# An expert's last short block computed beside a pair of its blocks, in one group of 320 columns

## The chip, the cores and the metric

The kernel runs on one core of a Trainium2 chip. The metric is the device time of one execution in microseconds (us), the median of several runs. A profile of one execution is shown beside it, with the work of the five engines: TensorE (PE, with its weight loads as PEld), VectorE (DVE), ScalarE (ACT), GpSimd (POOL) and SyncE (SP, which issues most of the DMA transfers).

## The reference

A linear attention gives 4608 tokens of 512 numbers, and a mixture of eight experts works on them. Each token goes to one expert only. The change touches the expert part alone.

```
# attention: phi(x) = [exp(p), exp(-p)], p = x @ w_phi - max|x @ w_phi|;  x: [4608, 512]
logits = x @ w_gate                      # [4608, 8]
expert_idx = argmax(logits, axis=1)
gate_w = softmax(logits)[expert_idx]
for e in range(8):
    xe = x[expert_idx == e]
    h = maximum(xe @ w1[e], 0)           # w1[e]: [512, 1024]
    out[expert_idx == e] = gate_w * (h @ w2[e])   # w2[e]: [1024, 512]
```

With the reference's inputs the eight experts get 759, 439, 659, 402, 373, 412, 536 and 1028 tokens. In blocks of 128 that is 6, 4, 6, 4, 3, 4, 5 and 9 blocks, 41 in all. The last blocks hold 119, 55, 19, 18, 117, 28, 24 and 4 tokens.

## The kernel before

The first 400 us compute the attention and write its rows to `x_dram`, with the routing of the first 27 of 36 token tiles done on the way. The expert that has most tokens by then is the "lead" expert: its weights are loaded first and its first three blocks are gathered early. Then the last nine tiles are routed (`route` with `final`). `place` works out on VectorE where each expert's blocks stand, `block_of` turns that into a block number per token, `tokens_of` finds the token of each place by 72 small matmuls into `pp`, and `experts_of` finds the expert of each block (`eidx`). `gather` fetches a block's token rows from `x_dram` by an indirect DMA, issued on GpSimd.

Every fp32 product is made of three matmuls of rounded parts: high by high, low by high and high by low. `weights(u, k)` splits one of eight weight pieces of unit `u` (k 0 to 3 of `w1`, 4 to 7 of `w2`): ScalarE casts `raw` to `wh`, then VectorE (or GpSimd for k = 3 and 7) subtracts and writes `wl`. `load_weights` loads the raw piece by SyncE, and skips the transfer if the next unit has the same expert. `x_parts` transposes a gathered block on TensorE into `px` and splits it into `xh` and `xl`.

Blocks are computed in units. A **pair** is two blocks of one expert, 256 tokens. Its first product (`pair_first`, four steps j) has the weights as the stationary operand and 256 token columns moving, 96 matmuls in all into `pm`. ScalarE then writes `hh` (ReLU, rounded) and VectorE `hl`. Its second product (`pair_second`) has 128 tokens stationary and 512 output columns moving, 48 matmuls into two banks `po`. A **single** is one block: 24 matmuls with 512 moving columns (`first_product`), eight transposes of the hidden values (`h_parts`, into `pht`), and 24 matmuls with 512 columns (`second_product`). `write` scales `po` by the token's gate value on ScalarE and scatters the rows by an indirect DMA.

There are 17 pairs and then 7 singles in a row, 41 blocks; two more singles run only if the count of blocks asks for them. The singles are software-pipelined by `step`. In the attention the order of each engine is written out by hand. In the expert part it is not: a scheduler places the instructions of each engine, starting from the order of the code, and each engine then works through its own list in order.

Of the kernel before, what the change touches and what calls it, by code (L numbers as in the profile page):

```python
# [19 lines left out]
P = 128  # L20
# [13 lines left out]
NPAIR = 17  # L34
NU = NB - NPAIR
NU_ALWAYS = NU - 2

NSLOT = 7
# [46 lines left out]
def tile_linear_attention_moe(  # L85
# [20 lines left out]
    gidx = keep.tile([P, NB], I32, name="gidx")  # L106
    sidx = keep.tile([P, NB], I32, name="sidx")
# [514 lines left out]
    spot = sg.tile([P, E], F32, name="spot")  # L622

    def place(pc):
# [4 lines left out]
        V.tensor_scalar(cni, cni, 6, 2, op0=ALU.arith_shift_right, op1=ALU.bitwise_and)  # L629
# [3 lines left out]
        even, odd2 = pe[:, 0], pe[:, 1]  # L633
        V.tensor_copy(odd2, cni)
        V.scalar_tensor_tensor(even, odd2, -0.5, nb, op0=ALU.mult, op1=ALU.add)
        spare = sg.tile([P, 1], F32, name="spare")
        V.tensor_reduce(spare, even, axis=AX.X, op=ALU.add)
        V.tensor_scalar(spare, spare, -1.0, 2.0 * NPAIR, op0=ALU.mult, op1=ALU.add)
        st8 = sg.tile([P, 2, E, E], F32, name="st8")
# [10 lines left out]
        V.scalar_tensor_tensor(over, over, -0.5, nb, op0=ALU.mult, op1=ALU.add)  # L650
        V.tensor_scalar(spare, spare, 0.0, None, op0=ALU.max)
        V.scalar_tensor_tensor(first, pst[:, 1], spare, pst[:, 0], op0=ALU.min, op1=ALU.add)
        V.tensor_scalar(paired, first, -1.0, 2.0 * NPAIR, op0=ALU.mult, op1=ALU.add)
        V.scalar_tensor_tensor(paired, paired, 0.0, over, op0=ALU.max, op1=ALU.min)
        V.tensor_tensor(singles, nb, paired, op=ALU.subtract)
        V.tensor_tensor(st8[:, 0], before, singles.unsqueeze(1).to_broadcast([P, E, E]), op=ALU.mult)
        V.tensor_reduce(start, st8[:, 0], axis=AX.X, op=ALU.add)
        V.tensor_scalar_add(start, start, 2.0 * NPAIR)
        V.tensor_tensor(spot, start, paired, op=ALU.subtract)
        V.scalar_tensor_tensor(spot, spot, 64.0, paired, op0=ALU.mult, op1=ALU.add)  # L660
        V.scalar_tensor_tensor(spot, spot, 64.0, first, op0=ALU.mult, op1=ALU.add)
# [222 lines left out]
    def lead():  # L884
# [13 lines left out]
        def pick_lead():  # L898
# [8 lines left out]
            V.tensor_scalar(key, iota_em, ld, -2.0 * E, op0=ALU.is_equal, op1=ALU.mult)  # L907
            V.tensor_tensor(key, key, iota_e, op=ALU.add)
# [177 lines left out]
    def block_of():  # L1086
        si_t = spots.tile([P, NTILE, E], F32, name="si_t")
        at = spots.tile([P, NTILE], I32, name="at")
        V.tensor_tensor(si_t, onehot, spot.unsqueeze(1).to_broadcast([P, NTILE, E]), op=ALU.mult)
        with nc.allow_low_precision("places are integers"):  # L1090
            V.tensor_reduce(at, si_t, axis=AX.X, op=ALU.add)

        late_at = spots.tile([P, NTILE], I32, name="late_at")
        turn = spots.tile([P, NTILE], I32, name="turn")
        V.tensor_scalar(turn, at, 6, 63, op0=ALU.arith_shift_right, op1=ALU.bitwise_and)
        V.tensor_single_scalar(late_at, at, 12, op=ALU.arith_shift_right)
        V.tensor_single_scalar(at, at, 63, op=ALU.bitwise_and)
        bi = spots.tile([P, NTILE], F32, name="bi")
        V.tensor_tensor(bi, blk, turn, op=ALU.is_ge)
        V.tensor_tensor(late_at, late_at, at, op=ALU.subtract)  # L1100
        V.tensor_tensor(bi, bi, late_at, op=ALU.mult)
        V.tensor_tensor(blk, blk, at, op=ALU.add)
        V.tensor_tensor(bi, bi, blk, op=ALU.add)
        for j0 in range(0, NTILE, 12):
            V.tensor_tensor(
                bsel[:, j0 : j0 + 12, :],
                iota_p[:, 0:NB].unsqueeze(1).to_broadcast([P, 12, NB]),
                bi[:, j0 : j0 + 12].unsqueeze(2).to_broadcast([P, 12, NB]),
                op=ALU.is_equal,
            )  # L1110

    def tokens_of():

        pp = ps_kv.tile([P, NB], F32, name="pp", tag="pk")
# [4 lines left out]
        emp = spots.tile([P, NB], F32, name="emp")  # L1119
# [3 lines left out]
    def experts_of():  # L1123
        ends = spots.tile([1, 2, E], F32, name="ends")
        G.tensor_tensor(ends[:, 0], first[0:1], paired[0:1], op=ALU.add)
        G.tensor_tensor(ends[:, 1], start[0:1], singles[0:1], op=ALU.add)
        V.tensor_reduce(nblk, ends[:, 1], axis=AX.X, op=ALU.max)
        eg = spots.tile([1, 2, NB, E], F32, name="eg")
        places = ((first[0:1], ends[:, 0], 0, 2 * NPAIR), (start[0:1], ends[:, 1], 2 * NPAIR, NB))
        for low, high, n0, n1 in places:  # L1130
            for j, edge in enumerate((low, high)):
                m = V.tensor_tensor(
                    eg[:, j, n0:n1],
                    iota_p[0:1, n0:n1].unsqueeze(2).to_broadcast([1, n1 - n0, E]),
# [5 lines left out]
        G.tensor_tensor(eg[:, 0], eg[:, 0], iota_e[0:1].unsqueeze(1).to_broadcast([1, NB, E]), op=ALU.mult)  # L1140
        with nc.allow_low_precision("experts are integers"):
            V.tensor_reduce(eidx, eg[:, 0], axis=AX.X, op=ALU.add)
# [6 lines left out]

    def blocks(u):  # L1150
        return [2 * u, 2 * u + 1] if u < NPAIR else [u + NPAIR]
# [40 lines left out]
    def x_parts(u, i):  # L1192
        if u >= lim[0] or i >= len(blocks(u)) or ("x", u, i) in st:
            return
        if i == 0:
            st["x", u] = [mp.tile([P, KD, 2 * P], F32R, name=n) for n in ("xh", "xl")]
        st["x", u, i] = True
        xg = st["xg", blocks(u)[i]]
        px = ps_x.tile([P, KD, P], F32, name="px")
        for k in range(KD):  # L1200
            turn(px[:, k, :], xg[:, k * P : (k + 1) * P])
        xh, xl = (x[:, :, i * P : (i + 1) * P] for x in st["x", u])
        A.copy(xh, px)
        V.tensor_tensor(xl, px, xh, op=ALU.subtract)
# [6 lines left out]
    def pair_first(u, j, half=None):  # L1211

        xh, xl = st["x", u]
# [146 lines left out]
    for u in range(1, NPAIR):  # L1360
        for j in range(4):
            pair_first(u, j)
            if j > 1:
                x_parts(u + 1, j - 2)
# [113 lines left out]
```

## Time and profile before

| | us |
|---|---|
| median of 3 runs | 904.98 |
| the runs | 902.72 to 909.48 |
| the profiled execution | 898.09 |
| its span, first to last instruction | 896.4 |
| TensorE busy in that span | 865.8 (97%) |
| ScalarE, VectorE, GpSimd busy | 608.0, 580.1, 487.1 |

A busy time is the union of an engine's instructions, so TensorE at 97% says that it hardly ever had nothing to do. It does not say how long one matmul holds it: a matmul's own duration (0.28 us for 256 columns) overlaps with its neighbours'. What a matmul costs is the distance from its start to the next one's start.

### The profile page before, as it was taken

The numbers are of one execution on the slowest core, as the hardware profiler recorded it, in microseconds if no ns is written. First come the engines' busy times: TensorE is split into PE (matmuls) and PEld (weight loads), VectorE is DVE, ScalarE is ACT, GpSimd is POOL, SyncE is SP. The second block draws the span as 40 slices with busy tenths as digits, with TensorE's granted clock in tenths as the row PEclk, the third lists the DMA queues.
The fourth block names the chain that finished last, engine by engine and source line by source line (L and its number), as shares of the span: only waits on it lengthen the run. The fifth ranks groups of instructions, "written<-read, shape, count | busy, mean of one in ns | idle before, by whom it ended". The sixth has DMA issues, their size and how long they took to land. (4 is left out here: it accounts for less than half of the span.)

```text
span 896.4 us, 18565 instructions
## 1 busy us (share of the span) xinstructions
PE 865.8 (97%) x6639; PEld 806.9 (90%) x6639; DVE 580.1 (65%) x1073; ACT 608.0 (68%) x954; POOL 487.1 (54%) x332
## 2 busy tenths in 40 slices
PE   7989999999999999989999999999999999999994
PEld 6989999999999999988899999999999999987883
DVE  7878789777978778677945444444454445557950
ACT  6969788988898879564655555555555555568951
POOL 6877677876787768532533333333343433345631
PEclk7999999999999999999999999999999999999998
DMA  6556655565646545560251253422535634653100
GB/s 209 154 159 196 201 186 158 173 198 185 184 153 201 185 133 159 166 210 14 96 170 66 96 165 118 164 72 89 164 119 158 215 119 119 243 198 110 47 25 15
DMA packets 81262, 129.73 MB, mean 145 GB/s; under 512 B 13006, under 2 KB 32974, under 8 KB 81168
## 3 DMA queue, kind: packets, MB, share of 16 engines
q1 hardware_dynamic: 73776, 107.58, 38.2%
q0 software_dynamic: 6720, 20.80, 7.4%
q8 instruction: 53, 0.87, 0.4%
q14 instruction: 41, 0.34, 0.1%
q10 hardware_dynamic: 672, 0.15, 0.1%
HBM read 136.81 MB, written 20.26 MB: 175 GB/s over the span
## 5 line engine op out<-in xcount | busy, mean ns | idle before, releaser
L59 DVE TENSOR_TENSOR wl<-raw,wh 128x1024 fp32r<-128x1024 f32 x138 | 184.2, 1347 | 134.4 <-ACT wh L59 134.4
L59 ACT CAST wh<-raw 128x1024 fp32r<-128x1024 f32 x184 | 191.3, 1051 | 92.0 <-PE po L59 64.4
L59 POOL TENSOR_TENSOR wl<-raw,wh 128x1024 fp32r<-128x1024 f32 x46 | 112.5, 2450 | 176.3 <-ACT wh L59 163.4
L59 PE MATMUL pm<-xh,wh 128*128 128x256 f32 x544 | 154.3, 284 | 2.7 <-DVE hl L59 2.7
L59 PE MATMUL pn<-kf,qp 128*128 128x73 f32 x1024 | 156.6, 253 | 0.0
L59 PE MATMUL pm<-xl,wh 128*128 128x256 f32 x544 | 154.8, 285 | 1.4 <-DVE xl L59 1.4
L59 PE MATMUL pm<-xh,wl 128*128 128x256 f32 x544 | 154.4, 284 | 0.0
L59 PEld LDWEIGHTS pn<-kf,qp 128*128 128x128 f32 x1024 | 151.1, 190 | 0.1
L59 PE MATMUL po<-wh,hh 128*128 128x512 f32 x328 | 131.4, 401 | 0.9 <-ACT hh L59 0.9
L59 PE MATMUL po<-wh,hl 128*128 128x512 f32 x328 | 128.1, 390 | 0.6 <-DVE hl L59 0.6
L59 PE MATMUL po<-wl,hh 128*128 128x512 f32 x328 | 128.5, 392 | 0.0
L59 POOL TENSOR_TENSOR kl<-e,kh 128x1024 fp32r<-128x1024 f32 x47 | 112.8, 2407 | 24.6 <-ACT kh L59 23.6
L59 DVE TENSOR_REDUCE mx<-ps_proj 128x4 f32<-128x512 f32 (+1 forms) x160 | 99.6, 634 | 34.7 <-PE ps_proj L59 33.7
L59 POOL TENSOR_TENSOR xl<-xr,xh 128x512 fp32r<-128x512 f32 (+2 forms) x63 | 93.1, 1482 | 51.8 <-ACT xh L59 31.1
L59 PEld LDWEIGHTS pm<-xh,wh 128*128 128x128 f32 x544 | 104.7, 193 | 5.3 <-DVE hl L59 2.8
L59 PEld LDWEIGHTS pm<-xl,wh 128*128 128x128 f32 x544 | 104.8, 193 | 4.2 <-DVE xl L59 1.7
L59 PEld LDWEIGHTS pm<-xh,wl 128*128 128x128 f32 x544 | 104.8, 193 | 0.0
L59 DVE TENSOR_TENSOR t<-ps_proj,mx 128x512 f32<-128x512 f32 (+1 forms) x160 | 97.8, 630 | 2.0
L59 POOL DMA_INDIRECT out<-ob,sidx x41 | 43.5, 1061 | 91.0 <-ACT ob L59 80.1
L59 ACT ACTIVATE e<-t 128x512 f32<-128x512 f32 (+1 forms) x160 | 85.4, 592 | 8.1 <-DVE kl L59 3.4
L59 PE MATMUL ps_proj<-w_hi,xh 128*128 128x256 f32 x288 | 84.1, 294 | 6.3 <-DVE t L59 3.1
L59 DVE SCALAR_TENSOR_TENSOR hl<-pm,hh 128x512 fp32r<-128x512 f32 x68 | 46.7, 687 | 61.5 <-ACT hh L59 61.5
(206 smaller groups left out, 1989.3 us busy)
## 6 DMA issues: line engine op xcount, KB each, us to landing
raw<-w SPq DMA_DIRECT2D x184, 512.0 KB
tq<-t SPq DMA_DIRECT2D x64, 256.0 KB
vt<-vv SPq DMA_DIRECT2D x15, 640.0 KB
x_dram<-xrow SPq DMA_DIRECT2D x30, 256.0 KB
xr<-kT SPq DMA_DIRECT2D x15, 320.0 KB
xr<-qT SPq DMA_DIRECT2D x15, 320.0 KB
xr<-kT SPq DMA_DIRECT2D x17, 256.0 KB
xr<-qT SPq DMA_DIRECT2D x17, 256.0 KB
```

Of the source, the lines that this page charges most:

```text
L59: m = f(*a, **kw)
```

## The change

The units have three forms now: nine pairs (`p`), six **trios** (`t`) and five singles (`s`) that always run, in the order that `FORMS` gives; eight more singles run only if there are more than 35 blocks beside the short ones.

A trio is a pair of an expert's blocks and that expert's last block, if that holds at most 64 tokens. The first product moves 320 columns instead of 256, one bank `pm` per 128 hidden rows (`trio_first`). In the hidden tile `h2` the columns stand so that the 64 high values of the short block and its 64 low values are neighbours. In the second product (`trio_second`) those 128 columns are one stationary operand: one matmul with `th` and one with `tl` give, in the lower 64 rows of `po2`, the high part's result, and in the upper 64 rows the low part's. `write_half` adds the two halves: ScalarE copies the upper half of `po2` to SBUF, a DMA moves it to the lower partitions, VectorE adds, ScalarE scales, and the scatter writes 64 rows.

```
+FORMS = "pp" + "p" * (NPLAIN - 3) + "tp" + "ts" * NONE_ALWAYS + "s" * (NONE - NONE_ALWAYS)
-NSLOT = 7
+NSLOT = 6
...
+    def trio_first(u, j):
+        xh, xl = st["x", u]
+        n = 2 * P + HALF
+        for i in range(2):
+            f = 2 * (j % 2) + i
+            pm = ps_h.tile([P, n], F32, name="pm")
+            for k in range(KD):
+                th, tl = (w[:, f * P : (f + 1) * P] for w in first_weights(u, j // 2, k))
+                T.matmul(pm, th, xh[:, k, :], start=(k == 0), stop=False)
+                T.matmul(pm, th, xl[:, k, :], start=False, stop=False)
+                T.matmul(pm, tl, xh[:, k, :], start=False, stop=(k == KD - 1))
+            h2 = hidden("h2", 2 * n)
+            A.activation(h2[:, 0:n], pm, AF.Relu)
+            for o, t, m in ((n + HALF, 0, 2 * P), (n, 2 * P, HALF)):
+                V.scalar_tensor_tensor(
+                    h2[:, o : o + m], pm[:, t : t + m], 0.0, h2[:, t : t + m], op0=ALU.max, op1=ALU.subtract
+                )
+            st["h2", u, 2 * j + i] = h2
...
+            both = h2[:, 2 * P : 3 * P]
+            T.matmul(po2, both, th[:, c], start=first, stop=False)
+            T.matmul(po2, both, tl[:, c], start=False, stop=last)
...
+    def write_half(b, po):
+
+        lower, upper = slice(0, HALF), slice(HALF, P)
+        ob = op.tile([P, DM], F32, name="ob", bufs=4)
+        A.copy(ob[upper], po[upper])
+        nc.sync.dma_start(ob[lower], ob[upper])
+        V.tensor_tensor(ob[lower], po[lower], ob[lower], op=ALU.add)
+        A.activation(ob[lower], ob[lower], AF.Copy, scale=gates[lower, b : b + 1])
+        scatter(b, lower, ob)
...
+        else:
+            first_product(u, 0)
+            x_parts(u + 1, 0)
+            tail(u - 1, 0)
+            x_parts(u + 1, 1)
+            tail(u - 1, 1)
+            x_parts(u + 1, 2)
+            ahead_weights(u, 0)
+            first_product(u, 1)
+            ahead_weights(u, 1)
+            h_parts(u, 0)
+            ahead_weights(u, 2)
```

`place` gets more steps: it finds which experts have a short last block and at least two full blocks to stand beside (four more for the lead expert), takes the first six, and places pairs, trios and singles. Its result per expert is two packed words instead of one, so `block_of` multiplies, sums and unpacks twice. `gates` keeps the gate values of all blocks (one small copy per block on VectorE), the transposed blocks use two fixed banks (`px0`, and `px1`, which `po2` shares), and six slots instead of seven hold the split pieces of `w2`.

The order that the scheduler made moves at three places.

On VectorE, ahead of the 72 matmuls `pp`: before, one word is formed (`spot`), multiplied and summed (`si_t`, `at`) and unpacked, and then `bsel` is compared.

```order
L59 SCALAR_TENSOR_TENSOR spot<-spot,first 128x8
L59 TENSOR_TENSOR si_t<-onehot,spot 128x288
L59 TENSOR_REDUCE at<-si_t 128x36
L59 TENSOR_SCALAR turn<-at 128x36
L59 TENSOR_SCALAR late_at<-at 128x36
L59 TENSOR_TENSOR bi<-blk,turn 128x36
L59 TENSOR_SCALAR at<-at 128x36
L59 TENSOR_TENSOR late_at<-late_at,at 128x36
L59 TENSOR_TENSOR blk<-blk,at 128x36
L59 TENSOR_TENSOR bi<-bi,late_at 128x36
L59 TENSOR_TENSOR bi<-bi,blk 128x36
L59 TENSOR_TENSOR bsel<-iota_p,bi 128x516 x3
```

Of the change, the end of the same stretch (`b_...` are the fields of the second word):

```order
L65 TENSOR_TENSOR b_6484<-b_6484,first 128x8
L65 SCALAR_TENSOR_TENSOR spot<-b_6488,b_6485 128x8
L65 TENSOR_TENSOR blk<-blk,low 128x36
L65 TENSOR_REDUCE nblk<-ends 1x1
L65 SCALAR_TENSOR_TENSOR spot<-spot,b_6484 128x8
L65 TENSOR_TENSOR words<-onehot,spot 128x288
L65 TENSOR_REDUCE at<-words 128x36
L65 TENSOR_SCALAR move<-at 128x36 x3
L65 TENSOR_TENSOR past<-past,move 128x108
L65 TENSOR_REDUCE bi<-past 128x36
L65 TENSOR_TENSOR bi<-bi,blk 128x36
L65 TENSOR_TENSOR bsel<-iota_p,bi 128x588 x3
```

From the first step of `place` to the first `bsel`, without the splits of weights and values that stand between, VectorE's list holds 45 steps before and 79 now. On TensorE, 11 more matmuls `po` of the first unit stand ahead of `pp`, and 5 instead of 16 between `pp` and the transposes of the next gathered block.

On VectorE, in a single: before, the splits of the weights (`wl`), of the hidden values (`hl`) and of the next block (`xl`) alternate.

```order
L59 TENSOR_TENSOR wl<-raw_6286,wh 128x1024
L59 TENSOR_TENSOR hl<-pht,hh 128x512
L59 TENSOR_TENSOR wl<-raw_6288,wh 128x1024
L59 TENSOR_TENSOR hl<-pht,hh 128x512
L59 TENSOR_TENSOR xl<-px,xh 128x4x128
```

Of the change, a single that follows a trio (`po_9375` is the bank `po2` of that trio, `h_9704` a hidden tile `h2` of the next one):

```order
L65 TENSOR_TENSOR xl<-px,xh 128x4x64
L65 COPY gates<-xg 128x1
L65 TENSOR_TENSOR wl<-raw_6298,wh 128x1024
L65 TENSOR_TENSOR wl<-raw_6292,wh 128x1024
L65 TENSOR_TENSOR ob<-po_9375,ob 64x512
L65 TENSOR_TENSOR hl<-pht,hh 128x512
L65 SCALAR_TENSOR_TENSOR h_9704<-pm,h_9704 128x256
L65 SCALAR_TENSOR_TENSOR h_9704<-pm,h_9704 128x64
```

The addition `ob`, which waits for the DMA of `write_half`, now stands between two weight splits and the `hl` that the single's second product needs. SyncE issues that DMA in its own list behind the loads of pieces 7, 3, 4 and 0 and ahead of that of piece 5.

On VectorE, at the end of the program, before:

```order
L59 TENSOR_TENSOR wl<-raw_6292,wh 128x1024
L59 TENSOR_TENSOR wl<-raw_6294,wh 128x1024
L59 TENSOR_TENSOR wl<-raw_6296,wh 128x1024
L59 TENSOR_TENSOR hl<-pht,hh 128x512 x4
```

and of the change:

```order
L65 SCALAR_TENSOR_TENSOR h_11261<-pm,h_11261 128x256
L65 SCALAR_TENSOR_TENSOR h_11261<-pm,h_11261 128x64
L65 SCALAR_TENSOR_TENSOR h_11278<-pm,h_11278 128x256
L65 SCALAR_TENSOR_TENSOR h_11278<-pm,h_11278 128x64
L65 TENSOR_TENSOR ob<-po_11159,ob 64x512
L65 TENSOR_TENSOR hl<-pht,hh 128x512 x2
```

The last trio's addition stands ahead of the last single's two `hl`. TensorE's list ends with the trio's last 16 matmuls `po`, 12 matmuls `pm` of the single, all eight transposes `pht` and 24 matmuls `po`; before, 24 matmuls `po` of the single ahead of it stood beside its transposes.

More of the change, by code (lines that the diff above doesn't have):

```diff
@@ L654, in place @@
         V.scalar_tensor_tensor(paired, paired, 0.0, over, op0=ALU.max, op1=ALU.min)
-        V.tensor_tensor(singles, nb, paired, op=ALU.subtract)
-        V.tensor_tensor(st8[:, 0], before, singles.unsqueeze(1).to_broadcast([P, E, E]), op=ALU.mult)
-        V.tensor_reduce(start, st8[:, 0], axis=AX.X, op=ALU.add)
+        V.tensor_scalar(first, first, room, None, op0=ALU.min)
+        V.tensor_tensor(singles, rest, paired, op=ALU.subtract)
+        ahead(start, singles)
         V.tensor_scalar_add(start, start, 2.0 * NPAIR)
-        V.tensor_tensor(spot, start, paired, op=ALU.subtract)
@@ L660, in place @@
-        V.scalar_tensor_tensor(spot, spot, 64.0, paired, op0=ALU.mult, op1=ALU.add)
-        V.scalar_tensor_tensor(spot, spot, 64.0, first, op0=ALU.mult, op1=ALU.add)
+        V.tensor_scalar(turn3, turn3, -2.0, 2.0 * NPAIR - 2.0, op0=ALU.mult, op1=ALU.add)
+        b1, b2, t2, t3, b3 = (sg.tile([P, E], F32, name=n) for n in ("b1", "b2", "t2", "t3", "b3"))
+        V.scalar_tensor_tensor(t2, has, 2.0, paired, op0=ALU.mult, op1=ALU.add)
+        V.tensor_tensor(b2, start, t2, op=ALU.subtract)
+        V.tensor_tensor(b1, turn3, paired, op=ALU.subtract)
@@ L1086, in block_of @@
     def block_of():
[L1087 to L1095, printed above, removed]
@@ L1096, in block_of @@
-        V.tensor_single_scalar(late_at, at, 12, op=ALU.arith_shift_right)
-        V.tensor_single_scalar(at, at, 63, op=ALU.bitwise_and)
+        words = spots.tile([P, NTILE, E], F32, name="words")
+        at = spots.tile([P, 2, NTILE], I32, name="at")
+        for i in range(2):
+            V.tensor_tensor(words, onehot, spot[:, i].unsqueeze(1).to_broadcast([P, NTILE, E]), op=ALU.mult)
+            with nc.allow_low_precision("places are integers"):
+                V.tensor_reduce(at[:, i], words, axis=AX.X, op=ALU.add)
@@ L1402, in step @@
             weights(u + 1, k)
-    for u in range(NPAIR, NU_ALWAYS):
-        step(u)
     rest = nc.values_load(nblk[0:1, 0:1], min_val=1, max_val=NB)
-    with tc.If(rest > NPAIR + NU_ALWAYS):
+    with tc.If(rest > 2 * NPAIR + NONE_ALWAYS):
         lim[0] = NU
```

257 lines of the change are left out of this document (184 added, 73 removed).

## The prediction

> **What bounds the kernel now.** I read the page's busy times and its 40 slices first, to see which engine sets the pace and where it does not.
>
> ```profile
> span 896.4 us, 18565 instructions
> PE 865.8 (97%) x6639; PEld 806.9 (90%) x6639; DVE 580.1 (65%) x1073; ACT 608.0 (68%) x954; POOL 487.1 (54%) x332
> PE   7989999999999999989999999999999999999994
> ```
>
> TensorE is busy for 90% or more of all slices but the first, the third, the eighteenth (381 to 403 us, where the last tiles are routed) and the last. So a matmul that goes away shortens the kernel, if nothing takes its place. Next I asked for the waits of TensorE from 450 to 885 us, the expert part after its start, and for busy times in two windows: 450 to 780 us, where only pairs run (the `pm` matmuls alone, columns PE, PEld, DVE, ACT, granted clock, DMA share, GB/s), and 794.4 to 884.9 us, where the singles run (POOL stands there too).
>
> ```profile
> PE po L59 <- ACT hh L59: 0.9, 1, 0.9
> PE po L59 <- DVE hl L59: 0.6, 1, 0.6
> PE pht L59 <- DVE hl L59: 0.2, 1, 0.2
> ...
> 450.00:780.00 330.00, 172.87 (x1368) 171.63 (x1368) 39.08 (x57) 33.45 (x56) 1.00 0.42 138
> 794.40:884.90 90.50, 88.84 (x429) 72.71 (x427) 59.33 (x52) 65.37 (x85) 46.35 (x25) 1.00 0.24 74
> ```
>
> TensorE waits 1.7 us in 435, at full clock. A pair has 96 `pm` matmuls, so a **pair** takes 330 / (1368 / 96) = 23.16 us. The second window starts behind the pairs' last `pm`: 12 `po` of the last pair, then seven singles. The other engines have slack in both windows, and ScalarE, the busiest, stands at 65.37 of 90.50.
>
> What one matmul costs is read from starts in TensorE's timeline: the first and last of 24 `pm` with 256 columns, a group of four transposes, and the first and last of 12 `pm` of a single with 512 columns.
>
> ```profile
> 782.77 0.28 PE L59 MATMUL pm<-xh,wh 128*128 128x256 f32 x1
> ...
> 785.52 0.28 PE L59 MATMUL pm<-xh,wl 128*128 128x256 f32 x1
> 785.64 0.45 PE L59 MATMUL px<-ident_r,xg 128*128 128x128 f32 x4
> 785.93 0.47 PE L59 MATMUL po<-wh,hh 128*128 128x512 f32 x1
> 786.24 0.40 PE L59 MATMUL po<-wl,hh 128*128 128x512 f32 x1
> ...
> 794.41 0.39 PE L59 MATMUL pm<-wh,xh 128*128 128x512 f32 x1
> 796.90 0.39 PE L59 MATMUL pm<-wh,xl 128*128 128x512 f32 x1
> ```
>
> With 256 columns the step is 2.75 / 23 = 0.1196 us, with 512 it is 2.49 / 11 = 0.2264 us: 0.000417 us for each column more, and about 0.013 us beside. Four transposes cost 0.29 us and the 0.08 by which the next matmul's step is longer, 0.37 us.
>
> **The change part by part.** *Removed:* two pairs, 2 x 23.16 = 46.3 us, and two singles. The window of singles has 88.84 us of TensorE work; without 12 `po` (2.72 us) that is 86.12 / 7 = 12.30 us each, 24.6 for two. Together 70.9 us.
>
> *Added:* six pairs become trios. A trio's 96 first matmuls move 64 columns more, 96 x 64 x 0.000417 = 2.56 us; it has 64 instead of 48 second ones, 16 x 0.2264 = 3.62 us; and one block more to transpose, 0.37 us. That is 6.55 us each, 39.3 for six. A step for 320 columns isn't in the trace: its ends are the 0.1196 of 256 and the 0.2264 of 512 columns. I take 0.1463 on the line between them, since the time per column is the same in the rows on both sides and 256 is the nearer one. TensorE's work falls by 70.9 - 39.3 = **31.6 us**.
>
> *What the other engines get.* These are the costs of one instruction in the groups by shape:
>
> ```profile
> L59 ACT CAST wh<-raw 128x1024 fp32r<-128x1024 f32 x184 | 191.3, 1051 | 92.0 <-PE po L59 64.4 <-PE pm L59 22.2 <-issue 2.6
> L59 DVE TENSOR_TENSOR wl<-raw,wh 128x1024 fp32r<-128x1024 f32 x138 | 184.2, 1347 | 134.4 <-ACT wh L59 134.4
> L59 DVE SCALAR_TENSOR_TENSOR hl<-pm,hh 128x512 fp32r<-128x512 f32 x68 | 46.7, 687 | 61.5 <-ACT hh L59 61.5
> L59 ACT ACTIVATE ob<-po,xg 128x512 f32<-128x512 f32 x41 | 28.2, 688 | 32.9 <-PE po L59 32.0 <-ACT ob L59 0.3
> ```
>
> A trio and the single behind it take TensorE 23.16 + 6.55 + 12.30 = 42.0 us. In it ScalarE has 16 casts (16.8 us), five output steps (at most 3.4) and the casts of blocks and hidden values, at 0.4 to 0.6 us each some 8 us by the `ob` row: about 28 of 42. VectorE has 12 weight splits (16.2), eight hidden tiles of 320 columns, by the 0.687 of 512 some 0.6 each (4.8), and about 6 us of the rest, about 27 of 42. The 41 copies into `gates` are single columns and lie in VectorE's idle time; on a VectorE that had none they would be some 0.15 us each, 6 us. The loads: the expert changes twelve times from one unit to the next instead of nine times, 12 MB more in all. Two of the nine fell between singles, 12.3 us apart, and ScalarE waited little for raw weights there:
>
> ```profile
> ACT wh L59 <- DMA raw<-w: 2.2, 2, 1.3
> ```
>
> That wait (780 to 896 us) held no matmul, and now a trio stands between two singles, so I cost the loads, the six slots and the `px` banks at nothing; without the cover, two waits of 1.3 us.
>
> *The start of the expert part.* VectorE's routing steps end in `gidx`, which the gather needs, and the gather feeds the transposes of block 3. TensorE had one gap of 0.27 us there:
>
> ```profile
> 412.33 0.17 DVE L59 SCALAR_TENSOR_TENSOR spot<-spot,paired 128x8 f32<-128x8 f32 x1
> 412.53 0.17 DVE L59 SCALAR_TENSOR_TENSOR spot<-spot,first 128x8 f32<-128x8 f32 x1
> 412.73 0.46 DVE L59 TENSOR_TENSOR si_t<-onehot,spot 128x288 f32<-128x288 f32 x1
> 413.71 0.18 DVE L59 TENSOR_SCALAR turn<-at 128x36 int32<-128x36 int32 x1
> 413.80 0.17 DVE L59 TENSOR_SCALAR late_at<-at 128x36 int32<-128x36 int32 x1
> ...
> 418.20 0.20 DVE L59 TENSOR_SCALAR gidx<-pp 128x43 int32<-128x43 f32 x1 [1.35 <-PE pp L59]
> ...
> 422.17 0.54 PE L59 MATMUL px<-ident_r,xg 128*128 128x128 f32 x4 [0.27 <-DMA xg<-x_dram,gidx]
> ```
>
> The list has 34 steps more. One that needs its neighbour's result takes 0.20 us (412.33 to 412.53), one that doesn't 0.09 (413.71 to 413.80): between 3.1 and 6.8 us. Two of them are of the size of `si_t`, 0.4 us more each. VectorE also waited twice in this stretch, for `xh` and `hh`, which takes some of it up:
>
> ```profile
> 410.07 0.69 DVE L59 TENSOR_TENSOR xl<-px,xh 128x512 fp32r<-128x512 f32 x1 [0.55 <-ACT xh L59]
> 411.53 0.69 DVE L59 SCALAR_TENSOR_TENSOR hl<-pm,hh 128x512 fp32r<-128x512 f32 x1 [0.69 <-ACT hh L59]
> ```
>
> At 0.12 us a step, since most added ones are interleaved with independent ones, this is 4.1 + 0.8 - 1.2 = 3.7 us later (ends 2 and 7). The 11 `po` moved ahead of `pp` don't help: they cover 2.5 us there, but from `gidx` to the transposes it is 4.0 us, and only 5 x 0.2264 = 1.1 us of matmuls are left for it. So **+3.7 us**, most of it in one gap of 2.8. What such a gap does to the clock is shown some us earlier, by a wait of 2.70 us and the window behind it (its last columns are granted clock, DMA share, GB/s):
>
> ```profile
> 403.49 0.58 PE L59 MATMUL pm<-xh,wh 128*128 128x256 f32 x1 [2.70 <-DVE hl L59]
> ...
> 403.40:406.40 3.00, 2.91 (x13) 0.50 0.16 10
> ```
>
> Thirteen matmuls at half clock, 2.91 us instead of 13 x 0.1196: 1.3 us lost. I add **+1.2 us** for this gap. The Trainium skill ("TensorE: Matmul & The Clock Gate", section "HAM oscillation — how this bites in real kernels") puts it that only gaps above some 3.4 us throttle; by that rule this term would be 0 and the sum 1.2 us lower. The row disagrees, 2.70 us was enough, and I go by the row.
>
> *The new wait.* `write_half` sends half a bank through a DMA, and VectorE and ScalarE stand in order behind it. Let a single start at 0. Its 12 `pm`, eight transposes and the trio's last 16 `po` end at 2.72 + 0.74 + 3.62 = 7.1 us; two `ob` and the copy, at most 0.688 each, end at 9.2. VectorE comes to the addition after two weight splits, whose casts stand behind the copy and a cast of half its size in ScalarE's list: 9.2 + 0.35 + 2 x 1.05 + 1.35 = 13.0 us. So the transfer has about 3.8 us of cover. Behind the addition wait `hl`, behind that the second product; TensorE comes to it at about 14.6, so what the transfer takes beyond its cover becomes idle time. The nearest row is the move of `t` to `tq`, SBUF to SBUF and issued by SyncE, 256 KB where this one is 128 KB; TensorE waited for it once:
>
> ```profile
> 48.62 0.48 SPq L59 DMA_DIRECT2D tq<-t  x1
> ...
> 52.66 0.54 PE L59 MATMUL pt<-ident_r,tq 128*128 128x128 f32 x4 [0.96 <-DMA tq<-t]
> ```
>
> That is 4.04 us in a busy stage, about the cover. If weight loads stand ahead of it in the queue it may take twice that, if the queue is empty less: 0 to 4 us in each of the four singles that have a trio on both sides. I take 0.8, **+3.2 us**. By the Trainium skill ("DMA: Bandwidth & Descriptors", section "Anatomy of one DMA — SWDGE (gpsimd) path") a transfer costs about 2.0 us and its bytes at 436 GB/s, an estimate of 2.3 us here, and the term would be 0; the section is on GpSimd's path, and the row above is nearer.
>
> *The end.* The last single has nothing behind it to fill its gaps. Call the end of its last `pm` E. The trio's `po` ended 2.72 us earlier, two `ob` and the copy at E - 0.7, the transfer by 4.04 us at E + 3.4, the addition and `hl` at E + 4.8. TensorE has 0.8 us of transposes and two `po` to do meanwhile, so it idles some 3.5 us; with a quick transfer about 2. I take **+3.0 us**, and 1.2 for the clock.
>
> Sum: -31.6 + 3.7 + 1.2 + 3.2 + 3.0 + 1.2 = **-19.3 us**. The profiled execution, 898.09 us, would become 878.8. It lies 6.9 us under the median of the runs shown, 904.98; the same step from the median gives **885.7 us**, my forecast.
>
> **The rivals.** *All gaps are covered.* The four waits come to nothing, as the 1.7 us of waits in 435 suggest for this schedule; against it, TensorE has only 5 `po` left behind `pp`. -31.6: 873.4 us.
>
> *The transfer is late.* VectorE and ScalarE stop for it. For it speaks that SyncE's queue carries 512 KB loads just ahead of it; against it, loads for a unit of the same expert are skipped, which holds for three of the five singles. With 4 us in each of four singles and 2 more at the end: -19.3 - 3.2 + 16 + 2 = -4.5, 900.5 us.
>
> *A matmul of 320 columns costs as much as one of 512*, slower than before. For it: no row has a width between the two. Against: one slope and one offset fit 256 and 512. The price is 6 x 96 x (0.2264 - 0.1463) = 46.1 us, so 27 us slower, 931.8 us; the kernel is slower from about 0.18 us per matmul on.
>
> *The conditional singles run.* The change then doesn't do what it says: if the routing finds no six short blocks, up to eight singles of 12.30 us follow, some 98 us. Against it: six experts have a last block of 4 to 55 tokens and at least two full ones, and what is left, 15 pairs and five singles, is exactly 35 blocks. The page's 41 scatters agree with the 41 blocks counted.
>
> **How the numbers follow.** A measurement of this kernel tells a difference of about 1%, 9 us. The forecast, a gain of 12 to 27 us, has a chance of 0.62; covered gaps 0.15; a late transfer 0.14, a third of which still ends above 1%; the slow matmul 0.06; the conditional part or something like it 0.03. Faster by over 1%: 0.62 + 0.15 + 0.05 = 0.82; within 1%: the other 0.09 of the late transfer and 0.02 of the last case, 0.11; slower: 0.06 + 0.01 = 0.07. The range reaches from the covered case to the late transfer: all waits at 0 give 873, a start of +7 us and 4 us in each single give 902, and the runs scatter by 3 to 4 us. With 870 to 900 us less than 2 in 10 is left out.
>
> **What the profile after would show.** Right: a step of 0.146 us in `pm` of 320 columns; about 29.7 us for a trio and 12.3 for a single; a gap of about 3 us at the transposes behind `pp` with the clock at 0.5 behind it; waits of VectorE for the DMA into `ob` under 1 us in the inner singles. Wrong: `ob` waits of several us, with TensorE idle ahead of `po`; TensorE waiting for `h2`, which would mean that the shorter `pm` groups come faster than ScalarE and VectorE empty them; more than 41 scatters (35 whole and six half ones).

## The result, and the profile after

The changed kernel takes **881.89 us** (median of four runs, 877.88 to 884.24) where the kernel before takes 904.91 (four runs, 902.72 to 909.48): a ratio of 0.9735 with a 95% interval of 0.9679 to 0.979. The forecast was 885.7 us with a range of 870 to 900. The profiled execution took 877.88 us, 20.2 less than the one before (898.09); the sum of the prediction said 19.3 less. That agreement is partly luck: the sections below show terms that were wrong and cancelled.

The page's first lines of the changed kernel:

```profile
span 876.1 us, 17931 instructions
PE 840.1 (96%) x6335; PEld 785.2 (90%) x6335; DVE 566.4 (65%) x1195; ACT 578.1 (66%) x936; POOL 479.8 (55%) x327
PE   8989999999999999998889999999999999999993
```

TensorE has lost 304 of its 6639 matmuls and 25.7 us of busy time and still sets the pace. There are more dips around the start of the expert part than before (slices 19 to 21, 394 to 460 us). All the rest of the difference can be found by cutting both spans at three matmuls that both programs have: the first `prk` (ranks of the last tiles, still the attention part), the first transpose `px` of the fourth unit (three pairs are computed by then in both kernels), and the last `po`. These are the rows of TensorE's timeline, first of before, then of after:

```profile
397.59 0.18 PE L59 MATMUL prk<-oh_b,ltri 128*128 128x48 bf16 x1 [0.63 <-DVE oh_b L59]
...
460.31 0.29 PE L59 MATMUL px<-ident_r,xg 128*128 128x128 f32 x2
...
884.51 0.39 PE L59 MATMUL po<-wh,hl 128*128 128x512 f32 x1
```

```profile
398.35 0.18 PE L65 MATMUL prk<-oh_b,ltri 128*128 128x48 bf16 x1 [0.53 <-DVE oh_b L65]
...
470.15 0.23 PE L65 MATMUL px<-ident_r,xg 128*128 128x128 f32 x1
...
861.43 0.39 PE L65 MATMUL po<-wh,hl 128*128 128x512 f32 x1
```

| stretch, us | before | before, again | after | after, again | after, third |
|---|---|---|---|---|---|
| start to `prk` | 397.6 | 396.8 | 398.4 | 399.8 | 400.0 |
| `prk` to `px` of unit 4 | 62.7 | 63.1 | 71.8 | 74.1 | 71.7 |
| `px` of unit 4 to the last `po` | 424.2 | 424.1 | 391.3 | 391.3 | 391.3 |
| last `po` to the end | 11.9 | 11.9 | 14.7 | 14.5 | 14.4 |

The columns marked "again" and "third" are repeated runs, described below. The pairs, trios and singles became 32.9 us shorter, the start of the expert part 9 us longer, and the stretch behind the last matmul 2.5 to 2.8 us longer. The first row differs between executions by some us whichever the kernel, which is why differences of 2 to 4 us are read below from `prk` on and not from the total.

Inside the trios the matmuls cost what was forecast. The first and last of 24 `pm` of 320 columns, and the first `pm` of two singles that follow each other with a trio between them:

```profile
781.29 0.30 PE L65 MATMUL pm<-xh,wh 128*128 128x320 f32 x1
...
784.66 0.31 PE L65 MATMUL pm<-xh,wl 128*128 128x320 f32 x1
```

```profile
761.17 0.39 PE L65 MATMUL pm<-wh,xh 128*128 128x512 f32 x1
...
803.19 0.39 PE L65 MATMUL pm<-wh,xh 128*128 128x512 f32 x1
```

3.37 / 23 = 0.1465 us a step, and 42.02 us for a single and a trio. In a window of 60 us in that part (busy time of TensorE, its weight loads, VectorE, ScalarE, GpSimd, then granted clock, DMA share, GB/s) TensorE is never idle:

```profile
700.00:760.00 60.00, 60.00 (x334) 53.45 (x333) 34.84 (x58) 35.21 (x49) 24.06 (x16) 1.00 0.59 200
```

The start is where the change gives time back. TensorE's waits from 396 to 472 us (total, times, longest), before and after:

```profile
PE pm L59 <- DVE hl L59: 2.7, 1, 2.7
PE pm L59 <- DVE xl L59: 1.4, 1, 1.4
...
PE px L59 <- DMA xg<-x_dram,gidx: 0.3, 1, 0.3
```

```profile
PE pm L65 <- DVE gates L65: 3.2, 1, 3.2
PE pm L65 <- DVE hl L65: 2.6, 1, 2.6
PE po L65 <- DVE wl L65: 1.8, 1, 1.8
PE pp L65 <- DVE bsel L65: 0.9, 1, 0.9
PE px L65 <- DMA xg<-x_dram,gidx: 0.8, 1, 0.8
```

Behind `prk`, 4.35 us of waits became 9.32. The granted clock makes up the rest. In windows of 3 us of the changed kernel (the third column from the right is the clock):

```profile
404.20:407.20 3.00, 3.00 (x14) 3.00 (x15) 3.00 (x17) 2.89 (x8) 1.72 (x3) 0.50 0.14 7
407.20:410.20 3.00, 3.00 (x17) 3.00 (x17) 0.93 (x10) 0.48 (x1) 0.00 (x0) 0.55 0.06 2
428.00:431.00 3.00, 3.00 (x10) 2.52 (x11) 0.69 (x1) 1.27 (x2) 2.60 (x4) 0.50 0.74 190
431.00:434.00 3.00, 3.00 (x17) 3.00 (x16) 0.56 (x2) 0.69 (x1) 1.58 (x3) 0.53 0.12 50
```

Two stretches at half clock lose 2.9 us each, 5.8 in all; before there was one, and it lost 1.6. So 5.0 us of waits and 4.2 of clock make up the 9.1 us, to 0.1.

Two causes of the longer waits stand in the rows. The first is on VectorE: the routing step `over` had its input at 408.1 us, but stood behind an `hl` whose `hh` was late, since TensorE ran at half clock:

```profile
410.35 0.69 DVE L65 SCALAR_TENSOR_TENSOR hl<-pm,hh 128x512 fp32r<-128x512 f32 x1 [2.23 <-ACT hh L65]
410.96 0.22 DVE L65 SCALAR_TENSOR_TENSOR over<-pst,spare,pe 128x8 f32<-128x8 f32 x1
...
423.90 0.21 DVE L65 TENSOR_SCALAR gidx<-pp 128x49 int32<-128x49 f32 x1 [0.86 <-PE pp L65]
...
432.30 0.50 DVE L65 TENSOR_REDUCE eidx<-eg 1x43 int32<-1x344 f32 x1 [2.20 <-POOL eg L65]
```

How much of this is the clock can be seen without an edit, since seven of the profiled executions have this start unchanged (the changed kernel three times, and no_hop, slow_hop, no_short and short_last below, which edit later parts). `gidx` came 25.5 us behind `prk` in the four where the clock was at half for 5.6 to 6.2 us behind the first gap, 24.7 in the two with 3.4 us of it, and 23.2 in the one where it did not drop (slow_hop). There VectorE doesn't wait at this `hl`:

```profile
410.49 0.68 DVE L65 SCALAR_TENSOR_TENSOR hl<-pm,hh 128x512 fp32r<-128x512 f32 x1
...
424.03 0.21 DVE L65 TENSOR_SCALAR gidx<-pp 128x49 int32<-128x49 f32 x1 [0.86 <-PE pp L65]
```

So of the 4.9 us by which `gidx` is later than before (20.6 us behind `prk`), 2.3 go with the clock and 2.6 with the longer list.

The second cause is on GpSimd: it issues four gathers before it comes to the three steps `eg` that the list of experts `eidx` needs (before: one gather, and `eidx` 4.75 us behind `gidx` instead of 8.40):

```profile
424.40 1.15 POOL L65 DMA_INDIRECT xg<-x_dram,gidx  x1 [8.02 <-DVE emp L65]
...
428.49 1.00 POOL L65 DMA_INDIRECT xg<-x_dram,gidx  x1 [0.30 <-issue]
429.51 1.57 POOL L65 TENSOR_TENSOR eg<-eg 1x440 f32<-1x440 f32 x2
```

### The profile page after: what moved, and what is told of

Its sections match the earlier page's. It is cut to its first block, busy times and chain, and to the rows that moved or that the text cites. A ratio compares the mean times of both kernels' runs of the same rounds, so it can differ in the third digit from the quotient of the medians.

```text
span 876.1 us, 17931 instructions
## 1 busy us (share of the span) xinstructions
PE 840.1 (96%) x6335; PEld 785.2 (90%) x6335; DVE 566.4 (65%) x1195; ACT 578.1 (66%) x936; POOL 479.8 (55%) x327
## 3 DMA queue, kind: packets, MB, share of 16 engines
q1 hardware_dynamic: 82960, 125.14, 45.6%
## 5 line engine op out<-in xcount | busy, mean ns | idle before, releaser
L65 DVE TENSOR_TENSOR wl<-raw,wh 128x1024 fp32r<-128x1024 f32 x114 | 158.1, 1401 | 108.8 <-ACT wh L65 106.3
L65 ACT CAST wh<-raw 128x1024 fp32r<-128x1024 f32 x152 | 157.3, 1052 | 93.3 <-PE po L65 68.8
L65 PE MATMUL pm<-xh,wh 128*128 128x256 f32 (+1 forms) x480 | 143.2, 299 | 2.6 <-DVE hl L65 2.6
L65 PE MATMUL pm<-xl,wh 128*128 128x256 f32 (+1 forms) x480 | 142.7, 298 | 3.2 <-DVE gates L65 3.2
L65 PE MATMUL pm<-xh,wl 128*128 128x256 f32 (+1 forms) x480 | 142.3, 297 | 0.0
L65 POOL TENSOR_TENSOR wl<-raw,wh 128x1024 fp32r<-128x1024 f32 x38 | 92.9, 2447 | 44.7 <-ACT wh L65 35.8
L65 POOL DMA_INDIRECT xg<-x_dram,gidx x41 | 52.7, 1284 | 112.9 <-issue 62.8
L65 PE MATMUL ps_proj<-w_hi,xl 128*128 128x256 f32 x288 | 82.6, 290 | 0.0
L65 PE MATMUL ps_proj<-w_lo,xh 128*128 128x256 f32 x288 | 82.0, 287 | 0.0
L65 PE MATMUL pk<-kl,vh 128*65 128x256 f32 x256 | 80.2, 313 | 0.6 <-POOL kl L65 0.6
```

Of the source, the lines that this page charges most:

```text
L65: m = f(*a, **kw)
```

## The experiments

All are edits of the changed kernel unless said otherwise. Theory: the gain is TensorE's columns alone, what is given back lies in VectorE's and GpSimd's lists at the start, and the transfer of half a bank is hidden. Rival: the transfer and the mix of trios and singles cost something, as the prediction had it.

### Repeated runs

> The changed kernel itself, run beside the others of this group on one chip, so that their times can be set against it. Expected: 0.97 to 0.98 of the kernel before, the start of the expert part (from the prk of the last tiles to the transposes of the fourth unit's first block) 9 us longer than in the kernel before, the rest to the last matmul 391.3 us long.

> The changed kernel itself, to have its time on the same chip as the other two of this group. Expected as before: 0.97 to 0.98 of the kernel before.

> The kernel before, unchanged, for a second profiled execution of it, since every number of before stands on one. Theory (the pieces are the program's, not one execution's): from prk to the transposes of the fourth unit's first block 62.7 us, within 1 us but for the clock, from there to the last matmul 424.2 us, within 0.3 us, and 11.9 us from the last matmul to the end of the span, 2.5 us less than in the changed kernel. Rival for the last: the end varies from one execution to the next, 12 to 15 us.

Measured: 878.75 us against 906.50 (ratio 0.969, interval 0.9648 to 0.9733) and 876.81 against 904.42 (0.9688, 0.965 to 0.9726); 897.53 for the one run of the kernel before. The medians lie 27.8 and 27.6 us apart here, 23.0 in the result above. The table above has their stretches. The third stretch repeats within 0.2 us, and the last one within 0.3. The start varies with the clock: 74.1 us in one of them, where the clock was also at half for 5.8 us behind the wait of the later `pm`. In the seven executions with this start it took 70.5 to 74.1 us.

### The experts' list on VectorE (eidx_vector)

```diff
-        G.tensor_tensor(eg[:, 0], eg[:, 0], eg[:, 1], op=ALU.subtract)
+        V.tensor_tensor(eg[:, 0], eg[:, 0], eg[:, 1], op=ALU.subtract)
...
+        if (u, i) == (1, 1):
+            behind(m, st["experts"])
```

(the two other `eg` steps likewise; `st["experts"]` is the step that writes `eidx`.)

> The changed kernel, but the three steps that make the list of experts out of eg run on VectorE instead of GpSimd, ahead of the block's xl. In the changed kernel GpSimd did them behind four gathers, and eidx came at 432.3 us of the span, 8.4 us after gidx (before: 4.8 us after). Theory (GpSimd's list makes the experts late, and with them the raw weights, and the late weight splits hold up the xl that TensorE waits 3.16 us for at 456 us): eidx about 4 us after gidx, ScalarE's waits for raw weights of 1.67 and 1.38 us gone, the gap of 3.16 us down to 1 or less; 2 to 3 us faster than the changed kernel. Rival (VectorE's own work is what is late there): the gap stays near 3 us, no difference above 1 us.

VectorE's row for `eidx`, and TensorE's waits from 396 to 472 us:

```profile
422.12 0.21 DVE L65 TENSOR_SCALAR gidx<-pp 128x49 int32<-128x49 f32 x1 [0.86 <-PE pp L65]
...
426.79 0.50 DVE L65 TENSOR_REDUCE eidx<-eg 1x43 int32<-1x344 f32 x1
```

```profile
PE pm L65 <- DVE hl L65: 2.6, 1, 2.6
PE po L65 <- DVE wl L65: 1.8, 1, 1.8
PE pp L65 <- DVE bsel L65: 0.9, 1, 0.9
...
PE px L65 <- DMA xg<-x_dram,gidx: 0.5, 1, 0.5
```

`eidx` comes 4.7 us behind `gidx`, and the gap of 3.2 us, which is 2.9 to 3.5 us long in all seven executions of the unchanged start, is gone. ScalarE's waits for raw weights, expected to go, are 1.8 us instead of 3.1. From `prk` to `px` it is 67.4 us, 4.4 less than in the changed kernel, of which some 3.5 are waits and the rest is clock. The time is 875.05 us against 899.65 (0.9733, 0.9697 to 0.9768), which is not told apart from the changed kernel's. So GpSimd's order was the cause of that gap in this program; what it is worth is seen from `prk` on, not in the total.

### The routing steps ahead (place_ahead, both)

```diff
+        if (u, j) == (0, 2):
+            behind(m, st["placed"])
...
+        if u == 0 and k in (KD, KD + 2, KD + 3):
+            behind(m, st["places" if k == KD + 3 else "placed"])
```

(`st["placed"]` is the last step of the first word, `m` the `hl` or the low part of a weight piece. `both` has this and the edit above.)

> The changed kernel, but on VectorE one hl and two weight splits of the first unit stand behind the steps of place that form the first word, not ahead of them. In the changed kernel VectorE stood 2.23 us idle at 408.1 us for the hh of that hl, with the next step of place, over, behind it. Theory (the chain of routing steps on VectorE sets when gidx comes, and what TensorE lacks there is time, not order): gidx 2 us earlier, at about 422; TensorE's gaps at pp, po and px (0.85 + 1.84 + 0.83 = 3.5 us) down to about 2, no half clock behind them; 3 to 5 us faster than the changed kernel. Rival (the weight splits that now come later make TensorE wait at po instead): the same gaps under other names, within 1 us.

> Both edits together: the experts' list on VectorE and the steps of place ahead. If the two costs are separate ones they add up: 5 to 8 us faster than the changed kernel, with its start of the expert part within 2 us of the kernel before. If one cause stands behind both (gidx late), no more than place_ahead alone, 3 to 5 us.

With the routing steps ahead, `gidx` came 23.5 us behind `prk` instead of 25.6, 2.1 earlier as expected; but the clock dropped for only 3.4 us behind the first gap here, and with that the unchanged start has 24.7. TensorE now waited elsewhere:

```profile
PE pm L65 <- DVE gates L65: 3.5, 2, 2.4
PE pm L65 <- DVE hl L65: 2.6, 1, 2.6
PE po L65 <- DVE wl L65: 2.5, 1, 2.5
```

From `prk` to `px` it is 70.5 us, which the unchanged start reaches too (70.5 to 74.1): a gain is not shown where 3 to 5 us were expected, and the rival was right. With both edits it is 66.0 us, 5.8 less than the changed kernel. That looks like the sum of the two gains, 4.4 and 1.3, and isn't. TensorE's waits are 6.6 us, longer than the 5.9 with the experts' list alone, since `po` waits 3.98 us for a `wl`; and the clock did not drop behind the first gap in this execution, which is worth some 1.7 us against that run. So whether the late routing steps cost anything of their own is not shown. The times, 879.29 (0.9759, 0.9684 to 0.9834) and 874.98 (0.9747, 0.9688 to 0.9806), don't tell them from the changed kernel.

### Splits on GpSimd (pool_lo)

```diff
-    POOL_LO0, POOL_LO = (1, 3), (3, 7)
+    POOL_LO0, POOL_LO = (1, 3, KD, KD + 2, KD + 3), (3, 7)
```

(and the experts' list on VectorE, and the `hl` behind the first word.)

> The changed kernel with three edits at the start of the expert part: the experts' list on VectorE, the hl of the first unit's third tile behind the first word of place, and the low parts of three pieces of the first w2 (0, 2 and 3) split by GpSimd, which is idle there, not by VectorE. Theory (VectorE's own list from place to gidx, with two weight splits of 1.2 us and a wait of 2.2 us in it, is the cost; nothing else there is short): gidx 4 to 5 us earlier than in the changed kernel, no gap of TensorE at pp, px and the later pm, 7 to 9 us faster than the changed kernel, about as fast at the start as the kernel before. Rival (GpSimd's splits take 2.4 us each and slow VectorE while they run, or come late for po): TensorE waits for wl instead, 4 to 5 us faster, as with the experts' list alone.

The theory failed: `bsel` came 24.2 us behind `prk`, later than in the changed kernel (22.6), and `prk` itself waited 2.1 us longer. The rival was near: from `prk` to `px` it is 67.8 us, about as with the experts' list alone, and GpSimd's splits slow VectorE while they run. Two steps of VectorE and the two splits of GpSimd beside them:

```profile
413.88 2.30 DVE L65 SCALAR_TENSOR_TENSOR paired<-paired,over 128x8 f32<-128x8 f32 x1
...
416.62 2.37 DVE L65 SCALAR_TENSOR_TENSOR spot<-first,t 128x8 f32<-128x8 f32 x1
```

```profile
413.75 2.41 POOL L65 TENSOR_TENSOR wl<-raw,wh 128x1024 fp32r<-128x1024 f32 x1 [1.88 <-ACT wh L65]
...
416.58 2.38 POOL L65 TENSOR_TENSOR wl<-raw,wh 128x1024 fp32r<-128x1024 f32 x1
```

A step on 8 numbers a row that takes 0.15 us takes as long as the whole split on the other engine, and then the next ones run at their usual pace. A third step beside a split on GpSimd, ahead of `prk` (`cand`, 2.29 us instead of 0.19), makes `prk` late. So a split of 1.2 us that moves to an idle GpSimd can cost VectorE up to 2.3 us. The Trainium skill ("Perfetto Trace Analysis", section "Optimizing Scalar/DVE Operations") says that the two share a port and that moving work between them might not help; this run agrees. The run took 876.39 us (0.9656, 0.9621 to 0.9691).

### VectorE's order written out (start_order)

Here the `hl` and the low part of piece 0 stand behind the first word and ahead of `words`, the low part of piece 2 and the first `xl` further back, the experts' list on VectorE; nothing moves to GpSimd.

```diff
+        if (u, k) == (0, KD):
+            behind(m, st["placed"])
+            st["first_low"] = m
+        if (u, k) == (0, KD + 2):
+            behind(m, st["first_low"])
...
+            m = V.tensor_tensor(words, onehot, spot[:, i].unsqueeze(1).to_broadcast([P, NTILE, E]), op=ALU.mult)
+            behind(m, st["first_low"])
...
+        if u == 1:
+            behind(m, st["experts" if i else "places"])
```

> The changed kernel with VectorE's order at the start of the expert part written so that the routing never waits: the steps of place that form the first word, then the hl that waits for hh, then the low part of piece 0 of w2, then words; the low part of piece 2 and the first xl behind that, the latter behind sidx; and the experts' list on VectorE. No work moves to GpSimd but back from it. Theory (what the start costs is VectorE's list alone): gidx 23.3 us behind prk (25.6 in the changed kernel), TensorE's waits at pp, po and px 1 us in all instead of 3.5 and no half clock behind them, no wait at the later pm; from prk to the transposes of the fourth unit's first block 63 to 65 us (71.8 in the changed kernel, 67.4 with the experts' list alone, 62.7 in the kernel before), so 7 to 9 us faster than the changed kernel. Rival (the splits that move come late for po, as in the run with place ahead): 67 us, no faster than the experts' list alone.

```profile
PE pm L65 <- DVE hl L65: 2.6, 1, 2.6
PE pm L65 <- DVE gates L65: 2.5, 1, 2.5
PE px L65 <- DMA xg<-x_dram,gidx: 0.8, 1, 0.8
...
PE po L65 <- DVE wl L65: 0.4, 1, 0.4
```

`gidx` came 23.1 us behind `prk` as expected, and the waits at `po` and `px` are 1.2 us with no half clock behind them. But the wait of the later `pm` is back with 2.5 us and 3.4 us of half clock behind it, although the experts' list is on VectorE; ScalarE waits 4.3 us for raw weights ahead of it, and why those are late here stays open. The stretch is 67.8 us where 63 to 65 were expected, of which some 1.2 us is the first gap's clock (nearly 6 us at half here, 3.4 with the experts' list alone). The run took **874.18 us** against 904.42 (0.9649, 0.9612 to 0.9685), the lowest ratio of those that compute all of it; the changed kernel on the same chip took 876.81. It beats the kernel before; that it beats the changed one, by 2.6 us with overlapping intervals, is not shown by the times.

### Without the transfer (no_hop), and with a slow one (slow_hop)

```diff
-        nc.sync.dma_start(ob[lower], ob[upper])
-        V.tensor_tensor(ob[lower], po[lower], ob[lower], op=ALU.add)
-        A.activation(ob[lower], ob[lower], AF.Copy, scale=gates[lower, b : b + 1])
+        A.activation(ob[lower], po[lower], AF.Copy, scale=gates[lower, b : b + 1])
```

> The changed kernel without the transfer of half a bank and without the addition behind it: the upper half of po2 is still copied, but the lower half alone is scaled and scattered (the product with the low values of the short blocks is left out of the output). Theory, from the trace of the changed kernel (TensorE never waits between 460 and 820 us, VectorE waits 0.2 us in all for the transfer): within 0.5 us of the changed kernel in the inner singles, at most 0.5 us less at the end. Rival, the terms of the prediction: 3.2 us less in four inner singles and 3 to 4 us less at the end, some 6 to 7 us in all.

From `px` of the fourth unit to the last `po` it is 391.1 us, 0.2 us less than with the transfer and the addition. The theory's number; the prediction's 6 to 7 us are not there. Time 878.94 us (0.9765, 0.973 to 0.98).

```diff
-        nc.sync.dma_start(ob[lower], ob[upper])
+        into, of = (ob[r].rearrange("p (b a c) -> a p b c", a=2, c=4) for r in (lower, upper))
+        for a in range(2):
+            nc.sync.dma_start(into[a], of[a])
```

> The changed kernel, but the half bank goes over in two transfers of 16-byte pieces instead of one of whole rows: same bytes, longer transfer. With L the time from its issue to VectorE's addition (3.6 us from issue to addition before, without a wait). Theory, read from one inner single of the changed kernel (issue at 769.4, addition at 773.0, TensorE needs the hl behind it at 776.3): up to L = 5.6 us costs nothing in the inner singles, every us beyond it costs one in each of the four, and at the end each us beyond 2.6 costs one; L = 8 would give some 9 to 15 us. Prediction's model: the same with 3.8 in place of 5.6, 7 us more at L = 8. Rival (the trio that follows gives the single enough other work): only the end becomes longer, by L - 2.6.

Time 908.99 us, 1.0026 of the kernel before (1.0001 to 1.0051): with this transfer the whole gain is gone. One of the four inner singles in the queue of SyncE, on VectorE and on TensorE, and the clock behind the gap:

```profile
737.75 4.91 SPq L1440 DMA_DIRECT2D ob<-ob  x2
...
748.44 0.68 DVE L65 TENSOR_TENSOR ob<-po,ob 64x512 f32<-64x512 f32 x1 [6.97 <-DMA ob<-ob]
...
749.77 0.51 PE L65 MATMUL po<-wh,hl 128*128 128x512 f32 x1 [4.94 <-DVE hl L65]
```

```profile
749.70:754.00 4.30, 4.23 (x12) 3.36 (x13) 2.87 (x7) 2.39 (x6) 0.94 (x1) 0.60 0.28 102
```

From issue to addition it is 10.69 us here and TensorE waits 4.94: 5.75 us are covered. The other inner singles give the same: 9.58 and 3.83, 10.49 and 4.75, 7.83 and 2.09, each 5.74 or 5.75. At the end it is 8.19 and 2.79: 5.4 covered, where the theory had 2.6. For the inner singles its 5.6 was nearly right, the prediction's 3.8 was not. The stretch grew by 30.5 us: 18.4 us of these five gaps, 1.6 at the first trio, and some 9.6 of half clock, 3 to 6 us behind each gap, which the expectation had left out; 0.9 us is left over.

### Without the short blocks' matmuls (no_short)

```diff
+                if k == KD - 1:
+                    T.matmul(pm[:, 2 * P :], tl, xh[:, k, 2 * P :], start=True, stop=True)
...
-            T.matmul(po2, both, th[:, c], start=first, stop=False)
-            T.matmul(po2, both, tl[:, c], start=False, stop=last)
+            if first or last:
+                T.matmul(po2, both, th[:, c], start=first, stop=last)
```

(and the three matmuls of a trio's `pm` take 256 columns.)

> The changed kernel with nearly all the short blocks' matmul work left out: the first products of a trio take 256 columns (one matmul of 64 columns per tile of 128 hidden values keeps the bank defined), and of the 16 second products of po2 only the first and the last are made. Everything else stays, the transposes, transfers, additions and scatters too. Theory (TensorE's columns set the time of the trios): 96 x 64 columns at 0.000417 us less 8 matmuls of 64 columns (0.3 us), and 14 x 0.2264 us: 5.4 us per trio, 32.6 us in all. Rival (ScalarE, VectorE or the loads come next within the trio and single's 42.0 us): less, with new waits of TensorE.

Time 853.76 us (0.9402, 0.9364 to 0.9441), 25.0 us less than the changed kernel on that chip; the stretch to the last `po` is 362.6 us, 28.7 less where 32.6 were expected. A single and a trio take 37.2 us (37.4 once) instead of 42.02, and TensorE waits for nothing in them, so its matmuls still set the pace with a tenth of that work gone. Why a trio gives 4.8 us and not 5.4 stands in TensorE's timeline: the matmul behind each of the 64-column ones starts 0.03 us after it, but the next one then starts 0.20 us later and not 0.12, or 0.32 and not 0.23 with 512 columns. All in all that is some 0.11 us for each of the eight where 0.04 was expected, 0.5 to 0.6 us a trio.

### A shorter last scatter (short_last)

```diff
-        scatter(b, slice(0, P), ob)
+        scatter(b, slice(0, 32 if b == blocks(NU_ALWAYS - 1)[0] else P), ob)
```

> The changed kernel, but the last single scatters 32 rows instead of 128 (96 rows of that block are left out of the output). From the last matmul to the end of the span it is 14.4 to 14.8 us in every run of the changed kernel and its variants, 11.9 us in the kernel before, whose last scatter moved 0.05 MB where the changed kernel's moved 0.26 MB. Theory (the rows of the last scatter make the difference): 12 to 12.8 us. Rival (what stands behind the scatter, the read of nblk and the branch, takes longer in the changed program): 14.5 us as before.

14.2 us, so the rows are not what makes the end longer (879.19 us, 0.9726, 0.9681 to 0.9772). The answer is in GpSimd's queue at the branch of the conditional part (duration in ns, shortest/median/longest), before and after:

```profile
L1408 POOLq EVENT_SEMAPHORE  x3: 17/17/43, 886.4 to 886.6; - x3
```

```profile
L1570 POOLq EVENT_SEMAPHORE  x5: 17/43/2387, 863.7 to 866.3; - x5
```

After the change GpSimd waits there 2.39 us, from 863.7 on, before it closes the program; the last scatter, issued at 862.82, lands 3.4 us later, at 866.2. Before it closed without that wait. With 32 rows the landing takes 2.9 us and the wait 1.9. The wait is in all twelve traces of the changed kernel and its variants (1.9 to 2.4 us) and in neither of the kernel before. Why the one program waits for its last scatter there and the other does not, these rows don't show.

## Why the prediction was right, and where not

- **The work, -31.6 us: right.** The 320-column step (0.1463 forecast) is 0.1465, a trio and a single 42.0 us as forecast. The stretch became 32.9 us shorter; the 1.3 beyond the sum is the 1.7 us of waits that the pairs and singles had, of which 0.45 are left.
- **The start, +3.7 and +1.2 us for the clock: too small, it is 9.1.** TensorE's waits at `pp`, `po` and `px` grew by 3.2 us, near the 3.7, but not by the mechanism of the forecast. `gidx` came 4.9 us later: 2.6 by the longer list, and 2.3 because VectorE stood behind an `hl` that the half clock made late, where the prediction let VectorE's waits take some of the chain up. Two steps failed. The first is the loads at nothing, as far as the start goes: the sum has no term for the list of experts that they wait for. The experts' list on GpSimd behind three more gathers made `eidx`, the weights and an `xl` late, 1.8 us more of waits at the later `pm`, and taking it off GpSimd removed that gap. The second is the clock, which cost 4.2 more and not 1.2: one more drop, and a longer first one, which is partly chance (3.1 to 6.2 us or none for the same gap).
- **The loads at nothing: right behind the start**, where TensorE waits 0.45 us in all and for no weights. They were counted one change of expert short, though: the queue of SyncE moved 17.6 MB more (125.14 MB on the page, 107.58 before), 0.8 of them the six transfers, so 16.8 MB of weights, four changes of 4.2 MB and not three.
- **The transfer in the inner singles, +3.2 us: wrong, it is 0.** The step that failed is the end of its cover. VectorE came to the addition 3.6 us behind the issue, near the 3.8 of the forecast, and in one single it did wait for the DMA:

```profile
731.31 0.68 DVE L65 TENSOR_TENSOR ob<-po,ob 64x512 f32<-64x512 f32 x1 [0.23 <-DMA ob<-ob]
```

That transfer, issued at 727.36, took 3.95 us to the addition (4.26 in the third execution), so the row of 4.04 was a fair size for it. But the prediction had TensorE come to the second product as soon as `hl` was done: the addition at 13.0 us of the single, TensorE at 14.6. Measured in the single at 761.17, the addition starts at 11.8 and TensorE needs the `hl` at 15.1, with 24 `pm` of the next trio ahead of that. So another 2.1 us are covered, 5.75 in all.
- **The end, +3.0 and +1.2: wrong, TensorE waits 0.45 us.** Two sizes were off here: the transfer was issued 1.7 us ahead of the end of the last `pm` (852.62 against 854.28) and not 0.7, since the two `ob` did not wait for the trio's last `po`, and it took 2.58 us in the quiet queue and not 4.04. So the addition starts 0.9 us behind the last `pm` and not 3.4. The Trainium skill's formula ("DMA: Bandwidth & Descriptors", section "Anatomy of one DMA — SWDGE (gpsimd) path"), an estimate of 2.3 us here, was nearer to that 2.58 us than the row. What the prediction didn't have is the 2.5 to 2.8 us behind the last matmul.
- **The sum:** -31.6 became -32.9, +4.9 became +9.1, +3.2 and +4.2 became nothing, and +2.8 was missing, with +0.8 in the attention part: -20.2 instead of -19.3.
- **The rivals:** 320 columns at the price of 512 and the conditional part are refuted by the rows; "all gaps covered" was right for two terms of four; the late transfer, put at 900.5 us, was made to happen with longer transfers than the rival's and gave 909.

## What to carry to other kernels

Cut both traces at instructions that they share, and compare the stretches before believing that a matching total proves the terms. Compare the clock in them too: one start took 70.5 to 74.1 us in seven executions, so an edit that is worth 1 or 2 us there can't be read from one trace. A transfer is covered until the bottleneck engine needs what stands behind it, not until the waiting engine gets to it. Where an engine's list ends in the indices of the next part, look at every other list that feeds that part (here the experts on GpSimd) and at what stands ahead of the chain waiting for something slower.

## What the hardware showed unexpectedly

**The clock after the same gap differs from one execution to the next.** In thirteen profiled executions TensorE waited 2.60 to 2.70 us for the same `hl`. The clock was at half behind it for 5.6 to 6.2 us in five, for 3.1 to 3.5 us in six, and not at all in two, of which one (the run with both edits) is here, beside the row of the changed kernel above that begins at 404.20:

```profile
406.40:409.40 3.00, 2.98 (x25) 2.99 (x26) 3.00 (x17) 2.94 (x9) 1.74 (x3) 1.00 0.15 7
```

25 matmuls in 3 us against 14. That alone moves a run by up to 3 us. The Trainium skill ("TensorE: Matmul & The Clock Gate", section "HAM oscillation — how this bites in real kernels") has gaps above some 3.4 us throttle. Here 2.09 us (in slow_hop) was enough, 2.61 us sometimes was not, and the changed kernel's 3.16 us at 456.06 was not.

What goes with the drop in these thirteen is where the gap falls. In the traces the granted clock changes only in steps of 3.41 us (the half stretches ahead of the last matmul are 3.41, 6.83 or 10.24 us long), and where the steps begin differs from one execution to the next. In the five, 1.4 to 2.0 us of the gap lay in one step and the other 0.6 to 1.2 in the next, which was at half already; in the six, at least 2.3 us lay in one step; in the two, the steps cut it into 1.03 and 1.58, and into 1.35 and 1.26. Of the 2.09 us that were enough 1.86 lay in one step, and the 3.16 us that were not were cut into 1.37 and 1.79. How much of a gap in one step is enough these traces don't settle: 1.44 us was, with short matmuls of the routing ahead of it in the same step, and the 1.58 us above were not. No run was made to test this.

**GpSimd's split of 128x1024 can hold a step of VectorE for its whole length**, 2.30 us where 0.15 is usual, even when the step has 8 numbers a row. Not every step is held: `t` out of `ps_proj`, 128x512, takes VectorE 0.68 us beside such long operations of GpSimd and without them. Which steps are held was not tested.
